# One key copy moved behind an ordering instruction, and one normalization moved from GpSimd to ScalarE, in a fused attention and gated-MLP kernel

## The chip, the cores and the metric

The kernel runs on one core of a Trainium2 chip. A core has five engines with a queue each: TensorE (PE, matmuls; its weight loads are listed as PEld), VectorE (DVE), ScalarE (ACT), GpSimd (POOL) and SyncE (SP, which here only starts transfers). Each engine takes its instructions in the order of the program; engines wait for each other by semaphores. The metric is the device time of one execution in microseconds (us); lower is better. It includes something around the span that the profile shows: the profiled execution took 442.84 us with a span of 441.0.

## The reference

The input is `q`, `k`, `v` of 8 batches, 8 heads, 576 rows, 64 columns, a number `tau`, and the weights of a gated MLP.

```python
scores = q @ k.T / 8
keep   = scores >= max(scores) - tau
attn   = softmax over the kept scores
x      = (attn @ v), heads side by side          # 576 x 512 for each batch
h      = relu(x @ w_in);  u, v = halves of h     # 576 x 512 each
v_n    = (v - mean) / sqrt(var + 1e-6)           # over the 512 columns of a row
gated  = u * (w_spatial @ v_n + b_spatial)
out    = gated @ w_out                           # 576 x 512 for each batch
```

## The kernel before

Heads are taken in pairs: 32 pairs (4 for each batch), and each pair of heads is cut into chunks of 128 query rows. That makes 18 *steps* for each batch. One step `g` computes the scores of both heads for one chunk (`scores`, then `scores_end`), their maxima (`top`), the exponentials (`spread`, `exps`, `mask`), and leaves the weights in `p`. A DMA transposes `p` to `pT`, and `pv` multiplies it with the values. When a batch's attention is done, its MLP follows in pieces between the steps of the next batch: `moe_v` (the half that is normalized, five row groups of 128, the last of 64), `moe_u`, `moe_s` (the spatial product, the gate), `moe_o`.

The order is written out by hand. `ORDER` is a list of tokens, one string for each of the first batches, the last one used again for the others; `run_token` turns each token into instructions, which go to the engines' queues in that order. The first batch begins with

```python
"L7:0 L8:0 S0:0 G0:0 Y0:0 Ci0:0 S1:0 M0:0 G1:0 Y1:0 QB1:0 L9:0 M1:0 F0:0 QA1:0 E0:0 ..."
```

`S` is `scores`, `G` is `turn_bank`, `Y` is `scores_end`, `M` is `top`, `E` and `F` are the exponentials of the two heads, `QB1` and `QA1` are the transposes of the keys and queries of pair 1 on TensorE (`qk_main`, L330), and `L` are loads.

Two heads share a PSUM bank in the middle of a step's scores. The last two matmuls of a step (`scores_end`, L715) may start only when an earlier one (`opened[g]`, the second matmul of `scores`, L706) is finished. This order is kept by an instruction in GpSimd's queue that does no work: `turn_bank` (L710) puts a `nop` there that waits for `opened[g]` and then signals; `scores_end` waits for the signal. In the profile it is `L712 POOLq EVENT_SEMAPHORE`. It is handled by GpSimd's sequencer, in its place in GpSimd's queue.

Before its transposes a pair's queries and keys are brought into another layout: `shape_qk(i)` (L188) copies each of them on GpSimd from the loaded tile (`ql`, `kl`) to `qn` and `kn` (L193). For pair 0 VectorE does it (`shape_first`, L199). For pair 1 it is called ahead of the first token (L1020), so its two copies stand in GpSimd's queue ahead of step 0's ordering instruction. Later pairs' copies come with the tokens `sq2`, `sq3` and so on. Pair 1's queries and keys are loaded in SP's queue after pair 0's.

After the last step the last batch's MLP has no more steps to lie between: `last_gmlp` (L795). It makes the five row groups of the half that is normalized (L804 to L821), raises their variances to the power -1/2 on GpSimd (L827, first groups 0 to 2, then 3 and 4), and then normalizes each group `d`: `nm` on VectorE (L836), then `vn = vrel * rstd + nm` (L838), for d = 0 and 3 on GpSimd, for 1, 2 and 4 on VectorE. Between the making and the normalizing stand `moe_u(Z, 0)` and `moe_u(Z, 1)`, and behind the normalizing `moe_u` 2 to 4 (L1059 to L1063), whose results ScalarE brings from PSUM to `uT` (L308). Then come the gate's matmuls, which read all five groups of `vn` (L848, L857), the gate's products on VectorE (L850, L860), and the output (L867 to L886).

Of the kernel before, what the change touches and what calls it, by code (L numbers as in the profile page):

```python
# [11 lines left out]
ALU = mybir.AluOpType  # L12
ACT = mybir.ActivationFunctionType
# [74 lines left out]
def kernel(  # L88
# [17 lines left out]
    nc = tc.nc  # L106
    B, H, S, D = q.shape
    assert (B, H, S, D) == (8, 8, 576, 64)
    scale = 0.125
# [75 lines left out]

    nat = {}

    def shape_qk(i):  # L188

        ts = []  # L190
        for w, nm in enumerate(("qn", "kn")):
            t = qkn.tile([P, 4, 2, D], F32, name=nm)
            nc.gpsimd.tensor_copy(  # L193
                out=t, in_=ld_ring[i // 2 % 2][w][:, 2 * (i % 2):2 * (i % 2) + 2].rearrange(
                    "p h c d -> p c h d"))
            ts.append(t.rearrange("p c h d -> p c (h d)"))
        nat[i] = ts

    def shape_first():  # L199

# [520 lines left out]
    def top(g, heads=slice(0, 2)):  # L721

        if on_act(g):
            nm = s_ring[g % 2][:, 704:706]
        elif g in negm:
            nm = negm[g]
        else:
            nm = negm[g] = small.tile([P, 2], F32, name="negm")
        h0, n = heads.start, heads.stop - heads.start
        dims = [[at[1] - at[0], n], [1, S]] if n > 1 else [[1, S]]  # L730
        nc.vector.tensor_reduce(out=nm[:, heads], in_=view(s_ring[g % 2], at[h0], dims), axis=AX.X,  # L731
                                op=ALU.max, negate=True)
# [62 lines left out]
    def last_gmlp(b):  # L795
# [35 lines left out]
        yield  # L831
        for d, rs in norms:
            n = P if d < 4 else 64
            eng = nc.gpsimd if d in (0, 3) else nc.vector
            nm = small.tile([P, 1], F32, name="nm")
            nc.vector.scalar_tensor_tensor(out=nm[:n], in0=mvs[d][:n, 0:1], scalar=-1.0,  # L836
                                           in1=rs[:n], op0=ALU.mult, op1=ALU.mult)
            eng.tensor_scalar(out=vn[:n, d, :], in0=vrel[d][:n], scalar1=rs[:n],  # L838
                              scalar2=nm[:n], op0=ALU.mult, op1=ALU.add)
        yield  # L840
        g = mw.tile([P, 4, S], BF16, name="gT")
        rows = out[b, 0:512, :].rearrange("(p c) n -> p c n", c=4)
# [85 lines left out]
    def run_token(tok, it):  # L928

        name, _, d = tok.partition(":")  # L930
        on_vector[0] = name[0] == "d"
        name = name[on_vector[0]:]
        b = it - int(d or 0)
        if (name, b) in done or b < 0:
            return
        kind = name.rstrip("0123456789")
        a = [int(x) for x in name[len(kind):]] if kind not in "SGYMHKBEFZW" else []
        g = 18 * b + int(name[len(kind):]) if kind in "SGYMHKBEFZW" else 0
        if b >= B or g >= len(steps):
            return  # L940
        if kind in ("B", "Z", "W") and on_act(g) == (kind == "W"):
            return
        i = 4 * b + a[0] if a else 0
        m = 2 * b + a[0] if a else 0
        if kind in "SGYMHKEFBZW":
            {"S": scores, "G": turn_bank, "Y": scores_end, "M": top, "E": lambda g: spread(g, 0),
             "F": lambda g: spread(g, 1), "H": lambda g: top(g, slice(0, 1)),
             "K": lambda g: top(g, slice(1, 2)), "B": shift, "Z": exps, "W": mask}[kind](g)
        elif kind in ("QA", "QB", "qa", "qb"):
            task("q", i, kind[1] in "Bb")[1 + (kind[0] == "q")]()  # L950
        elif kind in ("QR", "qr", "kd"):
            task("r", i)[1 + ("QR", "qr", "kd").index(kind)]()
        elif kind in ("sq", "sv"):
            (shape_qk if kind == "sq" else shape_v)(i)
        elif kind in "Pp":
            task("p", i, a[1])[1 + (kind == "p")]()
        elif kind in "Rr":
            task("pr", m)[1 + (kind == "r")]()
        elif kind in ("XP", "xp"):
            task("x", i)[1 + (kind == "xp")]()  # L960
        elif kind in ("RP", "rp"):
            task("t", m, a[1])[1 + (kind == "rp")]()
        elif kind in ("WS", "ws"):
            task("w", a[0])[1 + (kind == "ws")]()
        elif kind == "T" and (i, a[1]) == (NPAIR - 1, 1):
            turn_chunk(i, 3)
        elif kind == "T":
            turn_p(i, a[1])
            if (i, a[1]) == (NPAIR - 1, 0):
                turn_chunk(i, 2)  # L970
        elif kind == "TR":
            turn_rest(m)
        elif kind in ("X", "XR"):
            send_x(m, 8 if kind == "XR" else 4 if 2 * m in x_on_pe else 0, 9)
        elif kind == "L":
            load_of[b][a[0]]()
        elif kind[0] == "C":
            chores[kind[:2]][len(kind) == 3](a[0])
        elif kind == "OUT" and it == B - 1 and (name, b) not in held:
            held.append((name, b))  # L980
            return
        elif kind == "OUT":
            task("o", b, a[0])[3]() if a[0] < 4 else task("v", b + 1, 4)[6]()
        elif kind == "bv":
            task("v", b, a[0])[2](False)
        elif kind == "bs":
            task("v", b, a[0])[7]()
        elif kind in ("n", "k", "N"):
            task("v", b, a[0])[3 + "nkN".index(kind)]()
        else:  # L990
            task(kind[-1], b, a[0])[1 + (kind[0] == "e")]()
        done.add((name, b))
        on_vector[0] = False

    Z = B - 1
    with tc.manual_schedule():
        nc.vector.memset(warm, 1.0)
        for w in (0, 1):
            eng = (nc.sync, nc.scalar)[w]
            load(0, 1, w, eng)()  # L1000
            load_rest(0, w, 0, 2, eng)()
        make_identity(nc, identf)
        clear()
        nc.vector.memset(ntau, -float(tau))
        nc.vector.memset(mhalf, -0.5)
        nc.scalar.activation(out=ctau, in_=ntau, func=ACT.Exp)
        nc.vector.tensor_copy(out=identb, in_=identf)
        for w in (0, 1):
            load(1, 1, w)()
            load_rest(0, w, 2)()  # L1010
        load(0, 2, 2)()
        for w in (2, 3):
            load_rest(0, w)()
        for _ in range(8):
            nc.tensor.matmul(out=ps_f.tile([P, 512], F32, name="f").rearrange(
                "p (a b) -> p a b", a=4), lhsT=warm,
                rhs=warm.unsqueeze(1).broadcast_to([P, 4, P]), start=True, stop=True)
        shape_first()
        first()
        shape_qk(1)  # L1020
        load_of = [group_loads((b, 0)) + group_loads((b, 1)) for b in range(B)]
        for it in range(B):
            for tok in ORDER[min(it, len(ORDER) - 1)].split():
                run_token(tok, it)

        for tok in LAST.split():
            run_token(tok, B)
        for name, b in held:
            run_token(name, b)
        inner.close()  # L1030
        wide.append(ctx.enter_context(tc.tile_pool(name="ps_t", bufs=6, space=PSUM,
                                                  reuse_waits="tile")))
        due = []

        def run(*fs):
            for f in fs:
                f[1]()
                f[2]()
                for d in due:
                    d()  # L1040
                due.clear()
                if f[0] == "act" and len(f) == 8:
                    f[3]()
                    f[6]()
                    due.extend(f[4:6])
        def left(*names):

            return [task(t, n, f) for t, n, f in names if (f"{t}{f}", n) not in done]

        rest = left(("v", Z - 1, 4), ("u", Z - 1, 1), ("o", Z - 2, 0), ("u", Z - 1, 2),  # L1050
                    ("o", Z - 2, 1), ("u", Z - 1, 3), ("o", Z - 2, 2), ("u", Z - 1, 4),
                    ("o", Z - 2, 3))
        gates, outs = (left(*[(t, Z - 1, j) for j in range(n)]) for t, n in (("s", 5), ("o", 4)))
        if not rest:
            rest, gates, outs = gates + outs[:2], outs[2:3], outs[3:]
        run(*rest[:3], x_pe(NPAIR - 2), *rest[3:5], pv_rest(NPAIR // 2 - 1), *rest[5:6],
            pv(NPAIR - 1, 0), *rest[6:], pv(NPAIR - 1, 1), *gates[:2], x_pe(NPAIR - 1, True),
            *gates[2:])
        rest = last_gmlp(Z)  # L1059
        next(rest)  # L1060
        run(moe_u(Z, 0), moe_u(Z, 1))
        next(rest)
        run(*[moe_u(Z, j) for j in range(2, 5)], *outs)  # L1063
        next(rest)
        next(rest, None)
# [35 lines left out]
```

## Time and profile before

| | |
|---|---|
| median of 4 runs | 443.25 us (442.64 to 443.66) |
| the profiled execution | 442.84 us, span 441.0 us |
| TensorE busy | 413.4 us (94%) |
| VectorE busy | 394.3 us (89%) |
| ScalarE busy | 386.9 us (88%) |
| GpSimd busy | 179.4 us (41%) |
| copies of `qn` and `kn` on GpSimd (L193) | 0.61 us each at the start |
| normalizations in `last_gmlp` (L838) | VectorE 0.54 to 1.00 us, GpSimd 0.77 and 1.02 us |

A busy TensorE is not one at its peak, since matmuls overlap and their ends are modelled. In the views below, the order of time lists the start of an instruction, its length, engine, line, operation, what it writes and reads, how many were merged into the row, and in brackets how long its engine was idle before it and who ended that. Where the engine named there had long been done, something else ended the wait. The chain that ended last is followed back from the last instruction to what released it at each step. In the groups of instructions the two numbers behind the bar are the busy time of the group in us and the mean of one in ns, and then comes the idle time in front of the group.

### The profile page before, as it was taken

Reading aid. Unit: us, or ns where it says so; the run is one execution under the profiler, and the core shown is the slowest. Engines: PE = TensorE matmul, PEld = TensorE weight load, DVE = VectorE, ACT = ScalarE, POOL = GpSimd, SP = SyncE. Lnnn points to the kernel's source line nnn. Section 1 sums busy time; section 2 is a strip of 40 time slices with the busy share of each in tenths; the row PEclk is TensorE's granted clock in tenths of the full one; section 3 lists DMA queues with packets and bytes.
Section 4 is the critical chain, followed back from the end, with each engine's and each line's share of the span. In section 5 each row is a group of like instructions: output and inputs, shape, how many; then the busy total and the mean of one; then the engine's idle time right before and its main releaser. Section 6 shows DMA issues by size and latency. Waiting matters only on the chain.

```text
span 441.0 us, 12876 instructions
## 1 busy us (share of the span) xinstructions
PE 413.4 (94%) x5049; PEld 260.9 (59%) x5049; DVE 394.3 (89%) x641; ACT 386.9 (88%) x619; POOL 179.4 (41%) x384
## 2 busy tenths in 40 slices
PE   7677789999999999999999999999999999999995
PEld 4454555566655766666565666666566666555553
DVE  5988999998999898999999998999989998999782
ACT  3899799999899999999999989999899999999352
POOL 1445443860416511773146711574127711445031
PEclk9999999999999999999999999999999999999998
DMA  8999999889999999999999999999999998976923
GB/s 219 271 211 209 285 237 219 182 185 208 231 167 246 187 185 195 221 240 157 267 200 184 220 215 203 227 183 216 210 201 221 231 188 160 162 111 89 265 77 109
DMA packets 222588, 88.15 MB, mean 200 GB/s; under 512 B 193600, under 2 KB 218304, under 8 KB 222528
## 3 DMA queue, kind: packets, MB, share of 16 engines
q1 hardware_dynamic: 221872, 86.45, 95.0%
q8 instruction: 40, 0.66, 0.6%
q0 software_dynamic: 160, 0.52, 0.3%
q10 hardware_dynamic: 496, 0.36, 0.3%
q14 instruction: 20, 0.16, 0.1%
HBM read 32.79 MB, written 9.44 MB: 96 GB/s over the span
## 4 chain that ended last, share of the span: by engine, by line
DVE 36%; PE 35%; ACT 16%; issue 8%; DMA 3%; POOL 0%; POOLq 0%; DVEq 0%; ACTq 0%
PE s L697 15%; DVE s L731 13%; DVE p L761 9%; DVE negm L731 6%; ACT e L746 6%; ACT e L749 4%; ACT p L766 4%; PE f L595 3%; PE f L653 3%; DMA pT<-p 3%; PE f L382 3%; PE f L624 2%; DVE xn L391 2%; PE f L330 2%; DVE st L550 2%
## 5 line engine op out<-in xcount | busy, mean ns | idle before, releaser
L697 PE MATMUL s<-qkT 64*64 64x160 f32 (+1 forms) x2304 | 171.8, 415 | 14.8 <-ACT e L746 7.5
L697 PEld LDWEIGHTS s<-qkT 64*64 64x64 f32 x2304 | 106.7, 132 | 69.8 <-ACT e L746 17.4
L746 ACT ACTIVATE e<-s,negm 128x576 f32<-128x576 f32 x168 | 117.1, 743 | 12.3 <-DVE negm L737 8.0
L731 DVE TENSOR_REDUCE s<-s 128x2 f32<-128x1152 f32 (+1 forms) x91 | 115.3, 1268 | 10.3 <-PE s L697 8.9
L749 ACT ACTIVATE e<-s,negm 128x576 f32<-128x576 f32 x120 | 84.7, 748 | 10.7 <-DVE negm L731 9.5
L731 DVE TENSOR_REDUCE negm<-s 128x2 f32<-128x1152 f32 (+1 forms) x62 | 81.3, 1314 | 10.3 <-PE s L697 10.0
L761 DVE SCALAR_TENSOR_TENSOR p<-e,ctau 128x1152 bf16<-128x1152 f32 x60 | 85.6, 1429 | 1.2 <-ACT e L749 1.2
L766 ACT ACTIVATE p<-e 128x1152 bf16<-128x1152 f32 x68 | 79.0, 1171 | 0.4
L193 POOL COPY qn<-ql 128x512 f32<-128x512 f32 x31 | 25.4, 820 | 81.2 <-PE s L697 80.7
L382 PE MATMUL f<-v,pT 128*128 128x65 bf16 x1008 | 44.5, 194 | 0.0
L382 PEld LDWEIGHTS <-pT 128*128 128x128 bf16 x1024 | 41.4, 98 | 3.8 <-issue 2.2
L342 POOL COPY qkT<-qkT 64x64 f32<-64x64 f32 x32 | 7.9, 246 | 87.0 <-PE s L697 42.5
L391 DVE TENSOR_TENSOR xn<-f,r 128x256 bf16<-128x256 f32 (+1 forms) x93 | 35.4, 380 | 3.0 <-DVE r L389 0.2
L624 PE MATMUL f<-wsT,vn 128*128 128x512 bf16 x135 | 33.5, 380 | 0.4 <-ACT qkT L312 0.4
L595 PE MATMUL f<-xT,w_in 128*128 128x512 bf16 x120 | 29.8, 381 | 0.0
L377 PE MATMUL f<-v,pT 128*128 128x130 bf16 x126 | 27.7, 220 | 1.0 <-DVE xT L306 0.7
L580 POOL TENSOR_SCALAR vn<-vrel,rs,nm 128x512 bf16<-128x512 f32 (+1 forms) x35 | 26.8, 767 | 3.6
L530 PE MATMUL f<-w_in,xT 128*128 128x512 bf16 x112 | 27.5, 379 | 0.1
L312 ACT COPY qkT<-f 128x512 f32<-128x512 f32 (+1 forms) x56 | 24.4, 438 | 3.5 <-PE f L349 3.2
L653 PE MATMUL f<-w_o,gT 128*128 128x512 bf16 x100 | 24.8, 380 | 0.0
L216 POOL CAST v<-vl 128x512 bf16<-128x512 f32 x32 | 20.0, 624 | 10.3 <-PE s L697 9.4
L222 POOL CAST v<-vx 64x64 bf16<-64x64 f32 x64 | 20.9, 326 | 1.9
(166 smaller groups left out, 571.5 us busy)
## 6 DMA issues: line engine op xcount, KB each, us to landing
vl<-in_v_dram SPq DMA_DIRECT2D x16, 512.0 KB, 4.7
ql<-in_q_dram SPq DMA_DIRECT2D x15, 512.0 KB, 5.0
kl<-in_k_dram SPq DMA_DIRECT2D x15, 512.0 KB, 5.3
out_dram<-oo SPq DMA_DIRECT2D x12, 512.0 KB, 5.4
uT<-in_moe_w_in_dram SPq DMA_DIRECT2D x3, 512.0 KB, 4.8
uT<-in_moe_w_spatial_dram SPq DMA_DIRECT2D x2, 576.0 KB, 4.7
pT<-p SPq DMA_TRANSPOSE x65, 5.9
vx<-in_v_dram SPq DMA_DIRECT2D x16, 64.0 KB, 3.6
```

The lines of the kernel that those rows point to most:

```text
L377: nc.tensor.matmul(out=t[:, at:at + 130], lhsT=pt[:, 4, :], rhs=vt[:, 4:6, :].rearrange("p b d -> p (b d)"), start=True, stop=False)
L382: nc.tensor.matmul(out=t[:, at + 65 * h:at + 65 * h + 65], lhsT=pt[:, 5 * h + j, :], rhs=vt[:, 6 * h + j, :], start=False, stop=(h == 1 an ...
L391: nc.vector.tensor_tensor(out=dst, in0=o[ps, g0:g1, 0:64], in1=r[ps, g0:g1].unsqueeze(2).broadcast_to([ps.stop - ps.start, g1 - g0, 64]), ...
L595: nc.tensor.matmul(out=t, lhsT=w_in[:, m, f * P:(f + 1) * P], rhs=x_of(b, m, slice(0, 512)), start=(m == 0), stop=(m == 3))
L624: nc.tensor.matmul(out=t, lhsT=vn[:, c, f * P:(f + 1) * P], rhs=wsT[:, c, 0:512], start=(c == 0), stop=(c == 4))
L653: nc.tensor.matmul(out=t[:n], lhsT=gs[b][:, f, c * P:c * P + n], rhs=w_o[:, f, :], start=(f == 0), stop=(f == 3))
L697: made.append(nc.tensor.matmul(out=s_ring[g % 2][halves[k], at[h] + lo:at[h] + hi], lhsT=qks[n][halves[h], 0, m:m + 64], rhs=qks[n][halves ...
L731: nc.vector.tensor_reduce(out=nm[:, heads], in_=view(s_ring[g % 2], at[h0], dims), axis=AX.X, op=ALU.max, negate=True)
L746: nc.scalar.activation(out=e, in_=s, func=ACT.Prelu, bias=bias_, scale=scale if steps[g][1] == 4 else 1.0, alpha=1e30)
L749: nc.scalar.activation(out=e, in_=s, func=ACT.Exp, bias=bias_)
L761: nc.vector.scalar_tensor_tensor(out=numerators(g), in0=ef, scalar=ctau, in1=ef, op0=ALU.is_ge, op1=ALU.mult)
L766: nc.scalar.activation(out=numerators(g), in_=e_ring[g % 3].rearrange("p h s -> p (h s)"), func=ACT.Exp)
```

## The change

`shape_qk` gets an argument that says which of the two copies to make. Ahead of the first token only the copy of pair 1's queries is made; the copy of its keys is made right after the token `G0`, behind step 0's ordering instruction and ahead of step 1's. In `last_gmlp` the normalization of d = 3 becomes one activation (`Identity`, with scale and bias from memory) on ScalarE; it stands in ScalarE's queue behind the evictions of `moe_u` 0 and 1 and ahead of those of `moe_u` 2 to 4. The other four are as they were. On VectorE and SP the order of instructions is the same as before, and on TensorE too; there one weight load of the gate waits for ScalarE instead of GpSimd.

```diff
-    def shape_qk(i):
+    def shape_qk(i, parts=(0, 1)):
 
-        ts = []
-        for w, nm in enumerate(("qn", "kn")):
+        ts = nat.setdefault(i, [])
+        for w in parts:
+            nm = ("qn", "kn")[w]
             t = qkn.tile([P, 4, 2, D], F32, name=nm)
             nc.gpsimd.tensor_copy(
                 out=t, in_=ld_ring[i // 2 % 2][w][:, 2 * (i % 2):2 * (i % 2) + 2].rearrange(
                     "p h c d -> p c h d"))
             ts.append(t.rearrange("p c h d -> p c (h d)"))
-        nat[i] = ts
...
         for d, rs in norms:
             n = P if d < 4 else 64
-            eng = nc.gpsimd if d in (0, 3) else nc.vector
             nm = small.tile([P, 1], F32, name="nm")
             nc.vector.scalar_tensor_tensor(out=nm[:n], in0=mvs[d][:n, 0:1], scalar=-1.0,
                                            in1=rs[:n], op0=ALU.mult, op1=ALU.mult)
-            eng.tensor_scalar(out=vn[:n, d, :], in0=vrel[d][:n], scalar1=rs[:n],
-                              scalar2=nm[:n], op0=ALU.mult, op1=ALU.add)
+            if d == 3:
+                nc.scalar.activation(out=vn[:n, d, :], in_=vrel[d][:n], func=ACT.Identity,
+                                     scale=rs[:n], bias=nm[:n])
+            else:
+                (nc.gpsimd if d == 0 else nc.vector).tensor_scalar(
+                    out=vn[:n, d, :], in0=vrel[d][:n], scalar1=rs[:n], scalar2=nm[:n],
+                    op0=ALU.mult, op1=ALU.add)
...
              "K": lambda g: top(g, slice(1, 2)), "B": shift, "Z": exps, "W": mask}[kind](g)
+            if kind == "G" and g == 0:
+                shape_qk(1, (1,))
...
         first()
-        shape_qk(1)
+        shape_qk(1, (0,))
```

## The prediction

> **What bounds the kernel now.** I read the profile's page first, then the chain that ended last, then the order of time around the two edits.
>
> ```profile
> span 441.0 us, 12876 instructions
> ...
> DVE 36%; PE 35%; ACT 16%; issue 8%; DMA 3%; POOL 0%; POOLq 0%; DVEq 0%; ACTq 0%
> ```
>
> No engine alone is the bound: the chain hops between VectorE, TensorE and ScalarE nearly every microsecond, and GpSimd's share rounds to zero. Both edits touch GpSimd, so they are worth only what those few places on the chain hold. Both places exist. The first is the start:
>
> ```profile
> 6.68 1.74 PE s L697 x18
> 8.42 0.04 issue
> 8.46 1.37 DVE negm L731
> ...
> 22.50 1.25 PE s L697 x12
> ```
>
> The columns of this view are start, length, and what ran. Step 0's scores take 1.74 us from the first matmul to the release of VectorE's maximum; a later step on the same chain, undisturbed, takes 1.25. In the order of time one sees why:
>
> ```profile
> 6.51 0.61 POOL L193 COPY qn<-ql 128x512 f32<-128x512 f32 x1 [0.16 <-DMA ql<-in_q_dram]
> ...
> 7.72 0.61 POOL L193 COPY kn<-kl 128x512 f32<-128x512 f32 x1 [0.60 <-DMA kl<-in_k_dram]
> 7.83 0.51 PEld L697 LDWEIGHTS s<-qkT 64*64 64x64 f32 x16 [0.68 <-POOL qn L193]
> ...
> 9.25 0.66 PE L330 MATMUL f<-identf,kn 128*128 128x128 f32 x4
> ```
>
> ```profile
> L712 POOLq EVENT_SEMAPHORE  x1: 17/17/17, 7.7 to 7.7; - x1
> ```
>
> TensorE's weight loads stand still for 0.68 us in the middle of step 0. The row blames the copy of `qn`, but that ended at 7.12. What came at 7.7 is the ordering instruction of step 0 (L712), which stands in GpSimd's queue behind the copy of `kn`; that copy could not be issued before its load landed, just ahead of 7.7. The ordering instruction fires at the copy's issue (7.70), not at its end (8.33): so the load's landing is what is late, not the copy's 0.61 us.
>
> The second place is the last normalization, in the order of time:
>
> ```profile
> 425.29 0.87 ACT L308 ACTIVATE uT<-t 128x512 bf16<-128x512 f32 x2 [0.27 <-PE t L595]
> ...
> 426.00 0.21 DVE L836 SCALAR_TENSOR_TENSOR nm<-mv,rstd 128x1 f32<-128x1 f32 x2
> ...
> 426.25 0.54 DVE L838 TENSOR_SCALAR vn<-o,rstd,nm 64x512 bf16<-64x512 f32 x1
> 426.32 1.02 POOL L838 TENSOR_SCALAR vn<-vrel,rstd,nm 128x512 bf16<-128x512 f32 x1 [0.52 <-DVE nm L836]
> ...
> 427.40 0.94 PE L848 MATMUL t<-wsT,vn 128*128 128x256 bf16 x7 [0.49 <-POOL vn L838]
> ...
> 428.99 0.97 DVE L850 TENSOR_TENSOR gT<-f,uT 128x256 bf16<-128x256 f32 x2
> ...
> 431.46 0.58 ACT L869 COPY vl<-t 128x512 f32<-128x512 f32 x1 [5.30 <-PE t L867]
> ```
>
> Four of the five rows of `vn` are ready by 426.79; the gate's matmuls wait for d = 3 on GpSimd until 427.35. ScalarE is idle for 5.3 us in that stretch.
>
> **Part 1: the copy of `kn` behind the ordering instruction.** Nothing is added. One GpSimd copy (no DMA goes with it) is passed by one instruction that only waits and signals. That instruction now waits for the second matmul of step 0, which ends near 7.17, so it fires near 7.2. TensorE finds it done when its first twelve passes are issued (last start 7.36), and the step should run as an undisturbed one: 1.25 instead of 1.74, a gain of **0.49**. From below: if step 0's uneven start (half of `qkT` comes late) costs the last passes something more, 0.3; from above: the whole 0.68 of the stalled weight loads.
>
> Who pays: the copy of `kn` is issued when its load lands, as before, so it ends at 8.33 as before; its first reader is L330 at 9.25, which moves to some 8.76 and still finds it ready with 0.4 to spare. Behind the waiting copy in GpSimd's queue stands only step 1's ordering instruction, which needs step 1's first matmuls (near 7.95 after the change, the copy being issued at 7.7): no wait is created. If the load landed over 0.25 later, step 1 would take the stall that step 0 loses, hidden then by VectorE's 1.37 us maximum of step 0. Does the gain live for 430 us? The chain from 8.46 on passes through compute only, but for two waits on a DMA transpose near the end (5.2 and 6.4 us), whose issue waits for compute itself. The early loads that no compute moves have room: those of the next pairs land at 12.5 and 14.1 and are copied from 15.4 on; the value load of 17.5 is first used at 20.3. So the start's gain passes to the end whole.
>
> **Part 2: d = 3 on ScalarE.** Removed from GpSimd: 1.02. Added on ScalarE: one activation 128x512 from SBUF with a per-partition scale and a per-partition bias, a form that the trace does not have.
>
> ```profile
> L746 ACT ACTIVATE e<-s,negm 128x576 f32<-128x576 f32 x168 | 117.1, 743 | 12.3 <-DVE negm L737 8.0 <-DVE r L389 3.5 <-PE s L697 0.2
> ...
> L308 ACT ACTIVATE uT<-f 128x512 bf16<-128x512 f32 x20 | 11.9, 595 | 0.5 <-PE f L595 0.3
> L561 ACT ACTIVATE sq<-vrel,nmean 128x512 bf16<-128x512 f32 x16 | 11.6, 726 | 0.3
> ...
> L308 ACT ACTIVATE uT<-f 128x256 bf16<-128x256 f32 x2 | 0.7, 374 | 0.0
> ```
>
> The nearest row is L561: same source, same size, a bias from memory but no scale from memory: 0.73. The Trainium skill (ScalarE: Activation LUTs, What ACT_TABLE_LOAD costs) speaks against taking it as it is: each operand that points at a column costs some 93 ns more, on 186 ns and 0.833 ns an element, which is an estimate of 0.80 with two of them. The rows let one test the step: L308 grows by 221 ns for 256 elements, so 64 more are 55, and 743 - 595 - 55 leaves 93 for L746's one such operand. I take **0.80**; by the row alone it would be 0.73. Bounds: 0.60 (L308, no such operand) and 0.82 (L561 plus 93). No new table: a scaled copy (L310) uses the same function already, and the trace has one table load in all.
>
> The first of the two `nm` ends at 426.14. A hand-over from VectorE to ScalarE with a second wait takes 0.08 (chain at 19.24 to 19.32), so the activation runs 426.22 to 427.02, and TensorE resumes 0.05 later, at 427.07 instead of 427.40: a gain of **0.33** (by the row alone 0.40; bounds 0.31 to 0.53; d = 4, done at 426.79, does not let more through). VectorE's copy L664 ends at 427.38, ahead of the first gate product, now 427.57.
>
> Queued behind the new wait on ScalarE are the last three evictions of `uT` (before: 424.42 to 426.16). They now follow at 427.02 and end, at 0.60, 0.60 and 0.38, at 427.6, 428.2 and 428.6. Their readers: the third gate product at 428.66, the fourth at 429.2, the rest at 429.8. Each is covered by about 1 us, so they cost nothing; past that, every us late would be one on the chain. The next use of ScalarE is at 431.1.
>
> **Sum.** 0.49 + 0.33 = 0.82. The profiled execution took 442.84 (span 441.0 and 1.84 around it), so 442.02; it lies 0.41 below the median of the runs shown, 443.25, which becomes **442.43**, given as 442.4. One can tell a change of this kernel from none at about 0.2%, which is 0.89: times under 442.36 count as faster, over 444.14 as slower.
>
> **The rivals.**
> - *The start's gain is swallowed.* Some later stage waits for something that compute does not move, and only the end's 0.33 is left: 442.9. For it: the DMA engines are at nine tenths nearly all along. Against it: the chain has 3% DMA, and the transposes' issues wait for compute.
> - *More arrives.* The whole 0.68 at the start and an activation at 0.60 with 0.53 at the end: 1.21, so 442.0.
> - *Slower: the last transposes land late.* The chain holds
>
> ```profile
> 401.01 6.38 DMA pT<-p
> ```
>
>  and such a transpose takes a median of 5.9, but the one issued at 329.39 took 8.3, beside a load. If the shifted work makes this one meet other traffic and take 8.3, that is 1.9 more on the chain: 443.25 - 0.82 + 1.9 = 444.3. It decides from 1.71 on (0.82 + 0.89). For it: the spread of these landings. Against it: work and transfers shift together, so their distances stay.
> - *The change does not do what it says.* If the ordering instruction were late because of its matmul, part 1 would give nothing and the time be that of the first rival; the 7.2 against 7.7 speaks against it.
>
> **How the numbers follow.** Both gains arrive: 0.60, with a range of its own from 442.0 to 442.75; a little over half of it (0.34) lies under 442.36, since both upper bounds are farther off than the lower ones. Start swallowed: 0.13, same. More arrives: 0.14, faster. Late transposes: 0.13, slower. So faster 0.48, same 0.39, slower 0.13. The range for 8 in 10 goes from 441.5 (the most that both parts can give, 1.21, and the runs' own half us) to 443.6, which leaves the late transposes out.
>
> **What would show it.** In the changed kernel's profile: L712's first at 7.2, the maximum of step 0 starting at 7.98 instead of 8.46, the copy of `kn` still at 7.72, L330 near 8.8; at the end, counted from the same `nm`, an activation of 0.80 on ScalarE and L848 resuming 0.33 sooner. Wrong would make it: a later start of step 1 in place of step 0's, the lead of 0.49 gone by some 60 us, or a longer transpose near 401.

## The result

The changed kernel takes 442.47 us (median of 42 runs, 441.67 to 443.07), the one before 443.20. The ratio is 0.9979, with a 95% interval from 0.9974 to 0.9984: 0.93 us less, between 0.71 and 1.15. The ratio is taken over the runs and not from the two medians, which lie 0.73 apart; one of the 64 runs of the kernel before, at 996.96 us, is left out of it. The prediction was 0.82 less and 442.4. Run again beside three of the experiments, the changed kernel gave 0.9986 (0.9978 to 0.9994), 0.62 us less.

The profiled execution of the changed kernel, though, has a span of 440.8 us, only 0.26 less than before. To see why, one has to take it apart. First the chain that ended last (start, length, what ran):

```profile
6.90 1.24 PE s L697 x12
...
8.23 1.37 DVE negm L731
...
15.42 2.29 PE s L697 x12
```

Step 0's scores take 1.24 where they took 1.74: the predicted 1.25. But they begin at 6.90 instead of 6.68. The change does not touch what they wait for: the small loads for pair 0's last rows landed at 5.03 and 5.45 in this execution, at 4.62 and 4.35 in the other, and the transposes ahead of step 0 need them. Over all the profiles below, the start lies between 6.68 and 7.61, with a median of 6.89 in the old order of the copies and 6.90 in the new one. The third row is a surprise, and it is taken up below. In the order of time, and for step 0's ordering instruction (its last numbers are its first and last start):

```profile
7.56 1.22 PEld L697 LDWEIGHTS s<-qkT 64*64 64x64 f32 x20 [0.19 <-issue]
7.78 0.61 POOL L194 COPY kn<-kl 128x512 f32<-128x512 f32 x1 [0.55 <-DMA kl<-in_k_dram]
```

```profile
L712 POOLq EVENT_SEMAPHORE  x1: 17/17/17, 7.4 to 7.4; - x1
```

The 0.68 us gap in the weight loads is 0.19; the ordering instruction fires at 7.4, ahead of the copy of `kn`, which is issued at its load's landing as before.

The last normalization, in the order of time:

```profile
426.06 0.21 DVE L835 SCALAR_TENSOR_TENSOR nm<-mv,rstd 128x1 f32<-128x1 f32 x2
...
426.29 0.81 ACT L838 ACTIVATE vn<-vrel,nm,rstd 128x512 bf16<-128x512 f32 x1 [2.08 <-DVE nm L835]
...
427.01 1.33 ACT L308 ACTIVATE uT<-t 128x512 bf16<-128x512 f32 x3
427.16 0.94 PE L852 MATMUL t<-wsT,vn 128*128 128x256 bf16 x7 [0.20 <-ACT vn L838]
```

The activation takes 0.81 and the gate resumes 1.10 after the start of `nm`, where it was 1.40. The three evictions of `uT` behind it are done by 428.34; the first that uses one of them, the third gate product, starts at 428.75. They cost nothing.

The third row of the chain, 2.29 us for work that takes 1.2, is told by the busy times of two stretches (from and to, length, busy time and instructions of PE, PEld, DVE, ACT, POOL, then the granted TensorE clock, the DMA share and GB/s):

```profile
12.00:16.00 4.00, 2.29 (x29) 1.42 (x27) 3.97 (x6) 3.46 (x7) 1.08 (x3) 0.93 1.28 345
16.00:20.00 4.00, 3.96 (x35) 2.33 (x27) 3.43 (x5) 3.02 (x4) 1.93 (x4) 0.64 0.95 190
```

For 3.4 us from 15.44 on, TensorE had half its clock. The profile of before had no such spell. So the spans compare like this, each term being the difference between the two executions:

| from, to | before | after | difference |
|---|---|---|---|
| start to step 0's first score matmul | 6.68 | 6.90 | +0.22 |
| to the start of VectorE's maximum | 1.78 | 1.33 | -0.45 |
| to the last of `var` (L821) | 415.66 | 415.94 | +0.28 |
| to the gate's resuming | 3.29 | 2.99 | -0.30 |
| to the end | 13.63 | 13.61 | -0.02 |

Two of the five are the change, -0.75. The two positive ones, 0.22 and 0.28, look like the execution's own, which had to be tested.

### The profile page after: what moved, and what is told of

Read it like the earlier page. It is cut to its first block, busy times and chain, and to the rows that moved or that the text cites. A ratio compares the mean times of both kernels' runs of the same rounds, so it can differ in the third digit from the quotient of the medians.

```text
span 440.8 us, 12876 instructions
## 1 busy us (share of the span) xinstructions
PE 414.5 (94%) x5049; PEld 261.9 (59%) x5049; DVE 394.5 (90%) x641; ACT 387.6 (88%) x620; POOL 178.6 (41%) x383
## 4 chain that ended last, share of the span: by engine, by line
DVE 36%; PE 36%; ACT 17%; issue 8%; DMA 1%; POOL 0%; POOLq 0%; DVEq 0%; ACTq 0%
PE s L697 15%; DVE s L731 13%; DVE p L761 8%; DVE negm L731 6%; ACT e L746 6%; ACT e L749 4%; ACT p L766 4%; PE f L595 3%; PE f L653 3%; PE f L382 3%; DVE xn L391 2%; PE f L624 2%; PE f L330 2%; DVE st L550 2%; PE f L530 2%
```

## The experiments

The same stretches were read from the trace of every run. In the table, *step 0* is from its first score matmul to the start of VectorE's maximum (0.09 more than the chain's 1.24, which ends at the last matmul that the maximum needs), *middle* from there to the last of `var`, *gate* from there to the gate's resuming; *half clock* is the start of a spell of half the granted clock outside the last microseconds.

| profiled execution | step 0 begins | step 0 | middle | half clock | gate |
|---|---|---|---|---|---|
| before | 6.68 | 1.78 | 415.66 | - | 3.29 |
| before, again | 6.91 | 1.90 | 416.61 | 17.8 | 3.29 |
| after | 6.90 | 1.33 | 415.94 | 15.4 | 2.99 |
| after, again | 7.61 | 1.33 | 416.19 | 16.3 | 3.00 |
| copy alone | 7.36 | 1.33 | 415.66 | - | 3.28 |
| copy alone, again | 6.83 | 1.33 | 415.57 | - | 3.29 |
| normalization alone | 7.01 | 2.45 | 415.97 | - | 2.99 |
| normalization alone, again | 7.06 | 1.60 | 416.04 | 16.1 | 2.99 |
| load first | 6.83 | 1.40 | 415.58 | - | 3.29 |
| two copies | 6.89 | 3.05 | 416.50 | 19.1 | 3.29 |
| four copies | 6.72 | 3.76 | 416.24 | 11.3 | 3.29 |
| d = 0 on ScalarE | 7.02 | 1.33 | 415.99 | - | 2.84 |
| both on ScalarE | 6.69 | 1.33 | 415.58 | - | 2.63 |
| both on ScalarE, again | 6.80 | 1.33 | 415.65 | - | 2.63 |

### The copy alone

The change without its edit of the normalization.

```diff
+            if kind == "G" and g == 0:
+                shape_qk(1, (1,))
...
-        shape_qk(1)
+        shape_qk(1, (0,))
```

> Part 1 alone: the copy of kn behind step 0's ordering instruction, the normalization left on GpSimd. Theory (the start's gain passes whole): 0.49 us less than before, a ratio of 0.9989; step 0 takes 1.24 to 1.25 from its first matmul to the release of the maximum. Rival (a later wait swallows it): ratio 1.000 with the same 1.25 at the start, and VectorE's order of time level with before again by some 60 us.

Measured: ratio 0.9993 (0.9982 to 1.0004), which does not tell it from no change. The profile does: step 0 takes 1.33. From step 0's maximum to the last instruction, VectorE's instructions lie between 0.22 and 0.27 later than in the profile of before, a constant lag from an execution whose step 0 began 0.68 late and took 0.45 less. Nothing on the way takes the shift up.

> Part 1 alone again, since its first interval (0.9982 to 1.0004) did not tell it from no change. By the profiles so far a step 0 that waits for the ordering instruction takes 1.71, 1.83 or 2.38 us from its first matmul to the release, one that doesn't takes 1.26: theory 0.45 to 1.1 less in single executions, a ratio near 0.9988. Rival: within 0.9995 to 1.0005.

Measured: 0.9987 (0.9978 to 0.9996), 0.58 us less, an interval that leaves out no change. The start's gain reaches the end.

### The normalization alone

The change without its edits of `shape_qk`.

```diff
+            if d == 3:
+                nc.scalar.activation(out=vn[:n, d, :], in_=vrel[d][:n], func=ACT.Identity,
+                                     scale=rs[:n], bias=nm[:n])
```

> Part 2 alone: d = 3 on ScalarE, the copy of kn where it was. Theory: 0.3 us less than before (0.33 by the prediction, 0.29 by the changed kernel's profile), a ratio of 0.9993; step 0 takes 1.74 again, and the gate resumes some 1.10 after the start of d = 3's nm instead of 1.39. Rival (the evictions queued behind the activation cost something): ratio 1.000 or more.

> Part 2 alone again, for the same reason (0.9981 to 1.0002). The order of time of three profiles gives 0.30 us at the end: theory ratio 0.9993. Rival: 1.000.

Measured: 0.9991 (0.9981 to 1.0002), and again 0.9999 (0.9990 to 1.0009). By time alone part 2 was never told from no change. What it does in an execution is plain all the same: the gate resumes 2.99 us behind the last of `var` in both, as in both profiles of the changed kernel, and 3.28 or 3.29 in each kernel that leaves d = 3 and d = 0 where they were. That is 0.30, less than a time with this many runs can show.

The first of the two profiles shows something that the profile of before did not. Its chain:

```profile
7.61 1.09 issue
8.70 0.03 POOLq L712
8.73 0.14 issue
8.86 0.56 PE s L697 x8
```

Here the load of pair 1's keys landed at 8.67, a full microsecond later than in the profile of before, and step 0 waited for the ordering instruction until 8.7. With the copies in the old order step 0 takes 1.60, 1.78, 1.90 or 2.45 in four executions, for loads that landed at 7.87, 7.67, 8.02 and 8.67; in the new order it takes 1.33 in all seven, two of them with a landing at 8.4 or later. What part 1 is worth is therefore no fixed 0.45 but 0.27 to 1.12 by the execution. In the old order the length follows from the landing: in all four it is 0.79 more than the time from step 0's first matmul to the landing (0.81, 0.99, 1.11 and 1.66).

### Delaying the ordering instruction

The first run makes the copy four times, the second two times.

```diff
-            nc.gpsimd.tensor_copy(
+            for _ in range(4 if i == 1 and w == 1 else 1):
+              nc.gpsimd.tensor_copy(
```

> The kernel before with the copy of kn made four times in a row ahead of step 0's ordering instruction, so that this one fires at the issue of the last copy, three copies at 0.56 to 0.61 later: 1.7 us. Theory (a shift of the start passes to the end whole): 1.7 us more than before, a ratio of 1.0038. Rival (something later takes up a shift of the start): less than 1.0, a ratio under 1.002.

Measured: ratio 1.0062 (1.0048 to 1.0077), 2.75 us more; more than either theory gave. The chain:

```profile
9.06 0.61 POOL kn L194
...
9.72 0.03 POOLq L713
...
10.48 1.37 DVE negm L732
```

The copies follow each other at 0.67, since each waits for the one before, so three of them delay the instruction by 2.0 and not 1.7. In the profile, step 0 takes 3.76, 1.98 more than in that of before. VectorE's lag against that profile is 2.02 behind step 0, 2.58 behind a spell of half clock at 11.3, and then stays between 2.58 and 2.61 up to the end. So the delay passes whole, and the 0.56 arises where the clock is halved. That leaves the median, 447.05, which is 3.37 above before: five of its six executions were longer than the profiled one, and all six had a mean granted clock of 0.990 to 0.995.

> The kernel before with the copy of kn made twice ahead of step 0's ordering instruction. In the run with four copies each further one held the instruction back by 0.67 us, but the median was 3.4 us above before, 1.4 more than the 2.0 of the delay, with every execution at a granted clock of 0.990 to 0.995. Theory (the delay passes whole, the rest is the clock): 0.67 more than before in the order of time, ratio 1.0015 where the clock is as before. Rival (a late step 0 costs more than its delay by itself, in a later wait): the order of time shows a lag that grows after step 0 at a full clock.

Measured: 1.0015 (1.0004 to 1.0027), 0.66 us more for 0.67 of delay (by the interval, 0.2 to 1.2), with three of twelve executions at a low mean clock. The lag of its profile grows only in its spell at 19.1, and from 30 us on it is constant to 0.06. The theory holds: a shift at step 0 passes to the end. That a longer standstill of TensorE came with a low clock in six executions of six is taken up with the next run; only one of the six left a trace.

### Before once more: the clock

The kernel before, with no edit.

> The kernel before once more, for the granted TensorE clock of its executions. The profile of the changed kernel shows half the clock from 15.4 to 18.8 us, that of the kernel before does not. Theory (it falls on some executions of any kernel): executions of before come in the same groups of mean clock (0.994 and 0.997 to 0.999), those at 0.994 some 0.5 us longer. Rival (the earlier work brings it on): no execution of before at 0.994.

Measured: ratio to itself 0.9999 (0.9991 to 1.0007). Its profile has a spell of half clock at 17.8, and the middle is 416.61. So the spell comes without the change too. In the profiles, those with a spell have a mean granted clock of 0.994 or 0.995 and those without one 0.997 to 0.999, so that the mean tells the two apart. In the runs of before beside these experiments, 39 of 121 executions had a mean granted clock of 0.9965 or less (19 of 43, 11 of 43, 9 of 35), with medians of 444.06, 443.74 and 443.97 against 443.40, 443.25 and 443.28 for the others: 0.5 to 0.7 us. Of the changed kernel's first executions it was 16 of 43, at 442.56 against 442.22. Over all seven sets of runs with the new order of the copies (48 of 119 executions low) the same difference lies between -0.14 and 0.59, so 0.5 to 0.7 is what it was for the kernel before, and not a price for every kernel; why it is smaller there is open. The rival, that the earlier work brings the spell on, falls; that it makes it somewhat more frequent is neither shown nor excluded. In the table, the middle without a spell is 415.57 to 415.66 in six executions, and with one 415.94 to 416.61: 0.3 to 0.6 more where it starts at 15.4 to 16.3, 0.6 to 0.7 at 11.3, 0.8 to 1.0 at 17.8 and 19.1.

The traces also show where a spell comes from. In each of the six, the early spell and the one in the last microseconds start a whole number of 3.413 us apart (124 times it in five, 126 in four copies), so the clock is set on a grid of such windows, whose place differs from execution to execution. Here are the window ahead of a spell with four copies, and the one ahead of the spell and the spell itself in the changed kernel:

```profile
7.90:11.31 3.41, 1.44 (x22) 0.88 (x21) 0.83 (x1) 0.00 (x0) 2.27 (x4) 1.00 0.96 281
```

```profile
12.02:15.44 3.42, 1.71 (x26) 0.90 (x20) 3.42 (x4) 3.32 (x6) 0.52 (x2) 1.00 1.00 358
15.44:18.85 3.41, 3.41 (x30) 2.21 (x32) 3.17 (x4) 2.53 (x3) 1.40 (x3) 0.50 1.25 191
```

In the windows ahead of the six spells TensorE is busy for 38, 40, 42, 50, 50 and 50% (0.385 to 0.498); no other whole window of the fourteen executions, from 5 us on, is under 0.499, but for the last one, ahead of the spell at the end, with 0 to 41%. So a window in which TensorE is busy for less than about half is followed by one at half clock, as far as busy times with modelled ends can tell. The early steps have such a stretch between 12 and 19 us, and whether a window falls on it is the grid's chance. An estimate, by sliding the grid over the profile of before: 24% of its places give such a window with a bound of 0.49, 42% with 0.50, and 39 of 121 is 32%. With four copies it is three quarters by either bound, since the standstill makes a low window of its own, which goes with six of six; with two copies it is 42 to 58%, where three of twelve were low.

Two executions, one with the normalization alone and one with d = 0 on ScalarE, have 0.3 and 0.4 more in the middle without a spell. In each it arises in one place, where TensorE waited for a late transpose, the first issued at 300.70 and 6.91 us long, the second in the chain of d = 0 on ScalarE:

```profile
59.66 8.19 DMA pT<-p
```

### The load first

```diff
         for w in (0, 1):
             load(1, 1, w)()
+        for w in (0, 1):
             load_rest(0, w, 2)()
```

> The kernel before, with the load of pair 1's keys issued right behind that of its queries, ahead of the small load between them (0.65 us of SP's queue); the copy of kn stays ahead of step 0's ordering instruction. Theory (the landing of that load is what is late, not the copy's own time): the copy is issued some 0.65 sooner, the ordering instruction with it, and step 0 takes close to 1.25 instead of 1.74 in an execution like the one profiled before; time 0.3 to 0.5 less, ratio 0.999. Rival (the copy's 0.61 us has to be over first): the ordering instruction fires 0.61 after the copy's start and step 0 stays over 1.6.

Measured: 0.9994 (0.9986 to 1.0002). The order of time:

```profile
7.48 0.61 POOL L193 COPY kn<-kl 128x512 f32<-128x512 f32 x1 [0.32 <-DMA kl<-in_k_dram]
...
8.23 1.36 DVE L731 TENSOR_REDUCE negm<-s 128x2 f32<-128x1152 f32 x1 [1.55 <-PE s L697]
```

The load, issued 0.93 sooner than in the profile of before, landed only 0.24 sooner, at 7.43. Step 0 takes 1.40, 0.80 more than the time to the landing (0.60), with the copy still ahead of the ordering instruction and ending at 8.09: TensorE did not wait for its end. The theory (the landing is late, not the copy's own time) holds; the size of the move of the landing did not.

### d = 0 on ScalarE

In all profiles so far VectorE's normalization of d = 2 takes 1.00 us, though that of d = 1, of the same shape, takes 0.55. GpSimd's d = 0 runs beside d = 2, and the `nm` of d = 3 stands behind d = 2 in VectorE's queue. In the changed kernel:

```profile
425.09 0.77 POOL L841 TENSOR_SCALAR vn<-vrel,rstd,nm 128x512 bf16<-128x512 f32 x1
425.13 1.00 DVE L841 TENSOR_SCALAR vn<-vrel,rstd,nm 128x512 bf16<-128x512 f32 x1
```

```diff
-            if d == 3:
+            if d == 0:
...
-                (nc.gpsimd if d == 0 else nc.vector).tensor_scalar(
+                (nc.gpsimd if d == 3 else nc.vector).tensor_scalar(
```

> The changed kernel with d = 0 instead of d = 3 on ScalarE; d = 3 is on GpSimd again. Theory (GpSimd's d = 0 beside VectorE's d = 2 makes that one 1.00 instead of 0.55 and so holds back d = 3's nm, which stands behind it): d = 2 takes 0.55, and from the last of var (L821) to the gate's resuming 2.75 us instead of 2.99 in the changed kernel and 3.28 in the one before, though d = 3 takes 1.02 on GpSimd again; ratio 0.9977. Rival (VectorE's 1.00 has another reason): d = 2 stays at 1.00, the stretch is 3.28, ratio 0.9989.

Measured: ratio 0.9980 (0.9973 to 0.9987). Its d = 2:

```profile
425.31 0.55 DVE L841 TENSOR_SCALAR vn<-vrel,rstd,nm 128x512 bf16<-128x512 f32 x1
```

d = 2 takes 0.55, and the gate resumes 2.84 behind `var`: 0.45 sooner than before, though d = 3 takes 1.01 on GpSimd again. The expected 2.75 was 0.09 too little. The Trainium skill (GPSIMD Engine Reference, Key points) says that GpSimd shares its SBUF interfaces with VectorE and contends with those of its instructions that run in a two-port mode or read two inputs from SBUF. The pair of runs agrees that the two contend: 1.00 beside GpSimd's work, 0.55 without it. Which port mode VectorE ran in no trace shows.

### Both on ScalarE

```diff
-            if d == 3:
+            if d in (0, 3):
...
-                (nc.gpsimd if d == 0 else nc.vector).tensor_scalar(
+                nc.vector.tensor_scalar(
```

> The changed kernel with d = 0 on ScalarE as well; GpSimd normalizes none. Theory: d = 2 takes 0.55, d = 3's activation starts 0.45 sooner than in the changed kernel, and from the last of var to the gate's resuming it is 2.55 to 2.65 instead of 2.99, then bound by the matmuls ahead of the gate; some 0.4 less than the changed kernel, ratio to before 0.997. Rival (two activations in a row on ScalarE hold back each other or the evictions behind them): no better than the changed kernel.

> Both normalizations on ScalarE and the copy behind the ordering instruction again, for its interval: start as in part 1 alone and 0.67 at the end (its profile), so 1.1 to 1.3 less than before, ratio 0.9972. Rival (no better than the changed kernel): 0.998 to 0.9985.

Measured: 0.9977 (0.9967 to 0.9987), and again 0.9975 (0.9965 to 0.9984), 1.02 and 1.11 us less than before. The order of time of the first:

```profile
423.91 0.81 ACT L838 ACTIVATE vn<-vrel,nm,rstd 128x512 bf16<-128x512 f32 x1 [0.27 <-DVE nm L835]
...
424.57 0.55 DVE L841 TENSOR_SCALAR vn<-vrel,rstd,nm 128x512 bf16<-128x512 f32 x1
...
425.28 0.81 ACT L838 ACTIVATE vn<-vrel,nm,rstd 128x512 bf16<-128x512 f32 x1 [0.55 <-DVE nm L835]
...
425.91 1.26 PE L852 MATMUL t<-wsT,vn 128*128 128x256 bf16 x10
```

The first ten gate matmuls now run without a break: TensorE no longer waits there for `vn`. The gate's fourth matmul, the one that waited, starts 2.63 behind `var`, inside the expected 2.55 to 2.65. That is 0.36 sooner than in the changed kernel. The intervals of the two kernels' times overlap, so it is the order of time alone that shows it to beat the changed kernel.

### After once more

The changed kernel, with no edit.

> The changed kernel once more, beside the other three on the same chip. By the theory 0.8 us less than before, ratio 0.998; its own sum of parts is 0.49 at the start in an execution where the keys' load lands as in the profile of before, more where it lands later, and 0.3 at the end.

Measured: 0.9986 (0.9978 to 0.9994). In its profile the load of the keys landed at 8.43 and step 0 took 1.33 all the same; in the old order it would have waited at least to 8.4.

## Why the prediction was right

The forecast was 0.82 less; measured were 0.93 (0.71 to 1.15), and 0.62 (0.27 to 0.98) in the second set of runs. It lay on the edge between faster and same by the bound it set, 0.89, and so did the result, at 0.21%. That the sum came so close is in part luck: its 0.49 came from one profile, and the four profiles with the old order give part 1 between 0.27 and 1.12, 0.60 on average. With the 0.30 of part 2 that makes an estimate of 0.90.

- *Step 0 runs as an undisturbed one, 1.25 instead of 1.74.* Right: 1.24 in the changed kernel's chain, and 1.33 to the start of the maximum in all seven executions with the new order.
- *The copy and its reader do not suffer, step 1 gets no wait.* Right: the copy is issued at 7.78, the transposes at 9.00 find it done at 8.39, and step 0's maximum is followed by step 1's without a gap (8.23 and 9.51). The case of a late landing came too: with both on ScalarE the keys landed at 8.47, and step 1's weight loads stood still for 0.45 behind its ordering instruction; the two maxima still followed each other (8.02 and 9.30), so the stall was hidden as the prediction had it.
- *The start's gain passes whole.* Right, by the constant lag of the copy alone and by the delay with two copies, whose lag grew only in its spell of half clock. The rival that it is swallowed falls.
- *The activation takes 0.80.* 0.81. The two values ahead of it were 0.73 from the nearest row and 0.80 from the price for each operand in memory that the Trainium skill gives (ScalarE: Activation LUTs, What ACT_TABLE_LOAD costs); the measurement sides with the price, and with the upper bound worked from the rows, 0.82. There is one table load in the trace, as before.
- *The end gains 0.33.* 0.30: the hand-over took 0.10 and not 0.08, and the activation 0.01 more.
- *The evictions behind the activation are covered.* Right; they even end at 428.34 and not 428.6, since they overlap.
- *A late transpose.* The one issued near 401 took 6.4 to 6.5 us in every profile, so that rival did not come there. Its mechanism did, at other places and smaller: 0.3 and 0.4 us in two of the fourteen executions, by the transposes issued at 300.70 and 59.66.

What was not in the prediction is that the one profile of before was a mild case of the stall. The bound from above, the 0.68 of idle weight loads, was too low for a single execution: 1.12 was seen. The absolute marks it gave (7.98 for the maximum of step 0) missed by 0.25, because the start of step 0 moves from execution to execution between 6.68 and 7.61 with the landing of the first loads.

## What to carry to other kernels

An instruction that only keeps order inherited here every wait ahead of it in its queue; ask of each copy in front of it when its input lands, and put behind it what nobody needs yet. When a change of some tenths of a microsecond is judged, cut the trace into stretches at fixed instructions and compare those: here the end's stretch was the same to 0.01 us in every execution of the same code, and so was step 0's in the new order, while the whole time moved by more than half a microsecond for other reasons. Moving work off an engine can free a neighbour as well: d = 0 was never on the chain, and yet it set when d = 3 could begin.

## What the runs showed of the hardware

- A spell of 3.41 us at half the granted TensorE clock between 11 and 23 us, in six of the fourteen profiles and in five of the nine kernels, the one before among them; the middle is 0.3 to 1.0 us longer in those. Each follows a window of 3.41 us, on a grid of such windows, with TensorE busy for 38 to 50%.
- The ordering instruction in GpSimd's queue fired at the issue of the copy ahead of it (7.70 in the profile of before, with the copy running from 7.72 to 8.33), not at its end.
- VectorE's scaling of 128x512 from SBUF took 0.55 alone and 1.00 beside GpSimd's work of the same kind; that work took 0.77 beside d = 2 and 1.02 beside d = 4.
- An activation 128x512 from SBUF with scale and bias from memory took 0.81 each time.
- The landing of the same early load came between 7.6 and 8.7 us, issued between 3.3 and 3.6, in the thirteen profiles that left it in its place.
